# Loading the first 512 tokens' k and v four tokens to a partition, by head pairs, with their retention on 32-row groups of the array and states as 64x64 blocks

## The chip, the cores and the metric

The kernel runs on one core of a Trainium2 chip. The metric is the device time in microseconds (us) of one execution; lower is better. A run of the kernel before takes 208.84 us (median of three). The engines are named as the profile names them: PE is the matrix engine (PEld its weight loads), DVE the vector engine, ACT the scalar engine, POOL the general one, and SP the engine whose queue issues most transfers.

## What is computed

A retention layer (a linear recurrence over tokens) feeds a two-layer block with the Mish activation.

```python
B, H, S, D = 4, 8, 768, 64
gamma = 1.0 - 2.0 ** (-5.0 - np.arange(H))          # one decay per head
for t in range(S):
    state = gamma[None, :, None, None] * state + np.einsum('bhd,bhe->bhde', k[:, :, t], v[:, :, t])
    y[:, :, t] = scale * np.einsum('bhd,bhde->bhe', q[:, :, t], state)
x = y.transpose(0, 2, 1, 3).reshape(B * S, H * D)   # 3072 x 512
h = x @ w_in                                        # 512 x 2048
g = h * tanh(log(1 + exp(h)))
out = g @ w_out                                     # 2048 x 512, float32
```

## The kernel before, in words

**Tiling.** The 3072 tokens are 24 chunks of C = 128 tokens, six to a batch. Within a chunk the recurrence is done in closed form: *scores* (L266, the products of keys and queries), *mask* (L277, keeps the pairs in which the key is not later than the query), *present* (L317, the masked scores times v), *past* (L310, the queries times the state that earlier chunks left), *outer* and *state* (L288, L299, which make the state after the chunk). The powers of gamma are folded into the casts of q and v to float16, by a small constant table `qvs`. The eight heads go as HP = 4 pairs of 64 + 64 dimensions, so that a pair fills 128 partitions.

**Blocks.** The first block is four chunks (512 tokens of batch 0), the ten others are two chunks each. For each block, `g1` (L405) multiplies by w_in and ACT applies Mish; `g2_mm` (L424) or, from the third block of two on, `seven` (L486) multiplies by w_out. While block n is in g1 and g2, the retention of block n+1 is slipped between its matmuls at fixed places (`plan_of`, L646): `scores_two`, `outer_two`, `y_two`.

**States.** The state of a head pair is kept as a 128x128 block, of which only the two 64x64 blocks on the diagonal mean anything. `outer` makes it with one 128x128 matmul for each pair. `state` multiplies by `gcm`, which holds gamma^C in the two diagonal blocks and zero elsewhere, so the cross terms vanish. `past` is one 128x128 matmul for each pair.

**The first block.** Nothing can be put beside it: `first_block` (L570) writes its order out by hand. SP issues, in this order, two halves of q, then k and v of chunks 0 to 3 (eight transfers of 256 KB), then the weights w_in in six pieces (`load_weights`, L550), then w_out. The q of all 512 tokens is loaded four tokens to a partition (`load_first_q`, L177): partition p holds tokens 4p to 4p+3, 1 KB in a row for each head. k and v are loaded one token to a partition, 256 bytes in a row for each head (`load_one`, L120). Then, chunk by chunk, ACT casts k, POOL casts v, PE transposes k (L206), DVE copies the transposes out (L208), PE makes the scores (L273), DVE masks them (L283), and PE makes y (L313, L323) and the outer products (L291), with the state before added by a matmul against the identity (L296); DVE scales the state (L303) and ACT copies y into `xt` (L349, L358). Dummy matmuls (`spin`, L240, and `spin_quarters`, L247) keep PE working where it has nothing to do. After the last chunk come the casts of w_in on DVE (`cast_win`, L152) and then 64 g1 matmuls of 512 columns.

**What sets the order.** The program order on each engine is the order in which the code calls it (`manual_schedule`); an engine does not pass a waiting instruction. PSUM has four one-bank buffers under the tag "mm" and two two-bank buffers under the tag "at"; a new tile waits for the last reader of the tile whose buffer it takes.

The functions that the change touches and what calls them, with the line numbers of the profile:

Of the kernel before, what the change touches and what calls it, by code (L numbers as in the profile page):

```python
# [16 lines left out]
def kernel(  # L17
# [18 lines left out]
    CPB = TB // C  # L36
    BLOCKS = [4] + [2] * ((NCK - 4) // 2)
# [14 lines left out]
    spread = [qs_np[(jj * CPB + r) % C] for r in range(CPB)]  # L52
    qvs_np = np.ascontiguousarray(np.concatenate([qs_np, vs_np, *spread], 1))
# [5 lines left out]
    tpp = ctx.enter_context(tc.tile_pool(name="rn_tp", bufs=2))  # L59
# [12 lines left out]
    qvs = cpool.tile([P, (2 + CPB) * H], FP32, name="qvs")  # L72
    nc.scalar.dma_start(qvs, nc.inline_tensor(qvs_np, name="qvs_c").ap())
    qs, vs = qvs[:, :H], qvs[:, H:2 * H]
    qs_spread = qvs[:, 2 * H:].rearrange("p (r h) -> p h r", r=CPB)
    ident = cpool.tile([P, P], FP16, name="ident")
    tri = cpool.tile([P, C], FP32, name="tri")
    gcm = cpool.tile([P, HP, P], FP32, name="gcm")
# [10 lines left out]
    tri_first = cpool.tile([P, CPB, C // CPB], FP32, name="tri_first")  # L89
    nc.gpsimd.memset(tri_first, 0.0)  # L90
    nc.gpsimd.affine_select(
        out=tri_first, in_=tri_first, compare_op=ALU.is_gt, fill=1.0, base=0,
        pattern=[[-1, CPB], [-CPB, C // CPB]], channel_multiplier=1)
    nc.vector.memset(warm, 0.0)
    nc.scalar.activation(warm, warm, AF.Mish)
    nc.vector.memset(gcm, 0.0)
    for h in range(H):
        o = 64 * (h % 2)
        nc.vector.memset(gcm[o:o + 64, h // 2, o:o + 64], float(gamma[h] ** C))
# [4 lines left out]
    qfirst_t = cpool.tile([P, HP, CPB, P], FP16, name="qfirst_t")  # L104
# [9 lines left out]
    def room(g):  # L114
        loaded[g] = [
            None if nm == "q" and g < CPB else
            lpool.tile([P, H, D], FP32, name=nm + "f", tag=nm + "f", bufs=4 if nm == "q" else 6)
            for nm in "qkv"]
# [33 lines left out]
    def cast_win(s):  # L152
        src = wtmps.pop(("in", s))
        wins[s] = []
        for j in range(2):
            t = cpool.tile([P, NBP, TB // 2], FP16, name=f"win{s}_{j}")
            nc.vector.tensor_copy(t, src[:, :, j * (TB // 2):(j + 1) * (TB // 2)])  # L157
            wins[s].append(t)
# [18 lines left out]
    def load_first_q():  # L177

        qf = wstage.tile([P, H, CPB, D], FP32, name="qfirst", tag="wt", bufs=4)
        for a in range(0, H, H // 2):  # L180
            nc.sync.dma_start(  # L181
                qf[:, a:a + H // 2],
                q[0, a:a + H // 2, :TB].rearrange("h (p r) d -> p h r d", r=CPB))
        return qf

    def turn_first_q(qf, half, on_act):
        a, n = half * (H // 2), H // 2
        q16 = castp.tile([P, CPB, n, D], FP16, name="qfirst16", bufs=1, tag=f"qfirst16_{half}")
        nc.vector.tensor_tensor(
            q16.rearrange("p r h d -> p h r d"), qf[:, a:a + n],  # L190
            qs_spread[:, a:a + n].unsqueeze(3).broadcast_to((P, n, CPB, D)), op=ALU.mult)
        t_ps = mmps.tile([P, n // 2, CPB, P], FP16, name="t_ps", tag="mm")
        for i in range(n // 2):
            for r in range(CPB):
                nc.tensor.transpose(t_ps[:, i, r], q16[:, r, 2 * i:2 * i + 2], ident)
        dst = qfirst_t[:, a // 2:(a + n) // 2]
        if on_act:
            nc.scalar.copy(dst, t_ps)
        else:
            nc.vector.tensor_copy(dst, t_ps)  # L200

    def turn_k(g):
        k16 = cast[g][1]
        t_ps = mmps.tile([P, HP, C], FP16, name="t_ps", tag="mm")
        for i in range(HP):
            nc.tensor.transpose(t_ps[:, i], k16[:, 2 * i:2 * i + 2], ident)  # L206
        kt = qktp.tile([P, HP, C], FP16, name="kt", bufs=2)
        nc.vector.tensor_copy(kt, t_ps)  # L208
        qkts[g] = (qfirst_t[:, :, :, g * (C // CPB):(g + 1) * (C // CPB)], kt)

    def casts(g):
# [4 lines left out]
        if qf is not None:  # L216
            nc.gpsimd.tensor_tensor(  # L217
                q16, qf, qs.unsqueeze(2).broadcast_to((P, H, D)), op=ALU.mult)
# [18 lines left out]
    def at_tile(g):  # L237
        ats[g] = atps.tile([P, 2, HP, C], FP32, name="at", tag="at")

    def spin(g, n):  # L240
        for i in range(0, n, HP):
            m = min(HP, n - i)
            nc.tensor.matmul(  # L243
                ats[g][:, 0, :m], ident, ident.unsqueeze(1).broadcast_to((P, m, P)),
                start=True, stop=True)

    def spin_quarters(g, n, width):  # L247
        for i in range(n):
            r, c = i % 4 // 2, i % 2
            rows = slice(r * D, (r + 1) * D)  # L250
            nc.tensor.matmul(
                ats[g][c * D:(c + 1) * D, r, i // 4 % HP, :width], ident[rows, :D],
                ident[rows, :width], start=True, stop=True, skip_group_check=True)
# [12 lines left out]
    def scores(g):  # L266
        if g not in ats:
            at_tile(g)
        at, (qt, kt) = ats[g], qkts[g]
# [7 lines left out]
    def mask(g, parts=1):  # L277
        am = tpp.tile([P, 2, HP, C], FP16, name="am")
        at = ats.pop(g)
        keep = tri_first.rearrange("p r c -> p (r c)") if g < CPB else tri  # L280
        n = HP // parts
# [123 lines left out]
    def g1(blk, u):  # L405
# [15 lines left out]
        for j in range(per):  # L421
            gts[blk, u * per + j] = gt[:, j]
# [298 lines left out]
```

## Time and profile before

| | |
|---|---|
| runs | 208.76, 208.84 and 210.17 us; median 208.84 us |
| profiled execution, first to last instruction (span) | 206.5 us |
| its own device time | not listed beside the span; the median of the runs is 2.3 us above the span |
| busy: PE, PEld, DVE, ACT, POOL | 200.1, 151.0, 120.7, 86.5, 76.2 us |
| granted clock of PE, mean | 0.999 |
| k of chunks 0 to 3 landed, so that ACT could start its cast, at | 8.11 (behind other work of ACT), 10.36, 12.77, 15.13 us |
| first g1 matmul | 19.49 us |
| first matmul by w_out | 33.55 us |

Times inside an execution are counted from its first instruction. A line of the timeline has the start, the time, the engine, the line of the kernel, the operation, the tile written and those read, the shapes and the count; in brackets stands how long the engine had been idle and what ended that. The chain is the sequence of work that ended last, followed back from the last instruction. A matmul's time in a group is from its start to the end of its pipeline, so that a row of matmuls started one after another overlaps; the chain counts from the end of one group to the end of the next.

### The profile page before, as it was taken

The page shows a single profiled execution, that of the slowest core. Times are in us where ns is not written, and L with a number is a line of the kernel's source. Part 1 is how long each engine was busy: PE and PEld are TensorE (multiplying, and loading weights), DVE is VectorE, ACT ScalarE, POOL GpSimd, SP SyncE. Part 2 cuts the span into 40 slices and gives each one's busy share as a digit, 9 for nine tenths or more (in the row PEclk, how much of TensorE's full clock was granted, in tenths as well). Part 3 has the DMA queues.
Part 4 walks back from the last instruction along what each step waited for, and adds up shares of the span by engine and source line. Part 5 has one row for each costly group of instructions (what it writes and reads, how often), then busy time and mean ns, then how long its engine had stood idle before and what let it go on. Part 6 is the DMA issues. An engine that isn't in the chain of part 4 may idle for free.

```text
span 206.5 us, 4747 instructions
## 1 busy us (share of the span) xinstructions
PE 200.1 (97%) x2005; PEld 151.0 (73%) x2005; DVE 120.7 (58%) x184; ACT 86.5 (42%) x146; POOL 76.2 (37%) x72
## 2 busy tenths in 40 slices
PE   7899999999999999999999999999999999999993
PEld 2465444455855865788888888888888888898882
DVE  2697454267019998475585774495675773572062
ACT  2243664142631541453453453453453453552640
POOL 3242000427866555578665265156266000000000
PEclk9999999999999999999999999999999999999999
DMA  5999999999899999999999798499894800200202
GB/s 175 237 219 345 381 387 355 233 296 208 176 205 292 195 228 207 213 238 253 209 218 152 168 195 149 115 246 154 200 241 71 206 0 2 105 0 27 77 25 76
DMA packets 99988, 38.59 MB, mean 187 GB/s; under 512 B 90496, under 2 KB 94080, under 8 KB 99968
## 3 DMA queue, kind: packets, MB, share of 16 engines
q1 hardware_dynamic: 96704, 37.50, 82.4%
q10 hardware_dynamic: 3264, 0.81, 2.4%
q8 instruction: 15, 0.25, 0.5%
q14 instruction: 5, 0.04, 0.1%
HBM read 27.29 MB, written 6.29 MB: 163 GB/s over the span
## 4 chain that ended last, share of the span: by engine, by line
PE 83%; SPq 7%; DMA 5%; DVE 1%; ACT 1%; issue 1%; ACTq 0%
PE h_ps L412 38%; PE o_ps L506 23%; PE o_ps L426 13%; SPq L122 5%; DMA wi<-in_moe_w_in_dram 5%; PE y_ps L323 3%; PE at L273 3%; PE y_ps L313 2%; SPq L140 2%; PE u_ps L291 2%; ACT xt L400 1%; DVE gsum L476 1%; SPq L181 0%; DVE win L157 0%; PE t_ps L261 0%
## 5 line engine op out<-in xcount | busy, mean ns | idle before, releaser
L412 PE MATMUL h_ps<-xt,win 128*128 128x256 f16 (+1 forms) x704 | 88.0, 282 | 0.4 <-ACT xt L400 0.2
L420 ACT ACTIVATE g<-h_ps 128x512 f16<-128x512 f32 x96 | 57.3, 597 | 57.6 <-PE h_ps L412 57.6
L412 PEld LDWEIGHTS <-win 128*128 128x128 f16 x704 | 67.9, 98 | 16.9 <-DVE win L157 0.9
L217 POOL TENSOR_TENSOR qk<-qf,qvs 128x512 f16<-128x512 f32 x20 | 21.5, 1077 | 61.6 <-DMA qf<-in_q_dram 52.3
L283 DVE TENSOR_TENSOR am<-at,tri 128x1024 f16<-128x1024 f32 x20 | 23.7, 1220 | 17.1 <-PE at L273 16.9
L223 POOL TENSOR_TENSOR v<-vf,qvs 128x512 f16<-128x512 f32 x24 | 25.4, 1059 | 18.6 <-DMA vf<-in_v_dram 17.0
L426 PE MATMUL o_ps<-wout,g 128*128 128x512 f16 x128 | 30.1, 380 | 0.0
L222 POOL TENSOR_SCALAR qk<-kf 128x512 f16<-128x512 f32 x18 | 27.7, 1540 | 2.0 <-DMA kf<-in_k_dram 0.7
L506 PEld LDWEIGHTS <-gsum 128*128 128x128 f16 x256 | 24.4, 98 | 3.8 <-DVE gsum L476 0.4
L506 PE MATMUL o_ps<-tmat,gsum 128*128 128x256 f16 x192 | 23.7, 273 | 0.1
L426 PEld LDWEIGHTS <-g 128*128 128x128 f16 x128 | 11.7, 98 | 13.0 <-issue 0.3
L520 DVE TENSOR_TENSOR osb<-o_ps,snap 128x256 f32<-128x256 f32 x24 | 10.1, 422 | 18.8 <-ACT snap L512 15.7
L506 PEld LDWEIGHTS <-g 128*128 128x128 f16 x192 | 18.8, 98 | 2.2
L400 ACT CAST xt<-y_ps 128x1024 f16<-128x1024 f32 x10 | 10.1, 1012 | 21.7 <-PE y_ps L323 21.7
L475 DVE TENSOR_TENSOR gsum<-g 128x512 f16<-128x512 f16 x16 | 7.6, 472 | 13.6 <-ACT g L420 13.6
L506 PE MATMUL o_ps<-wout,g 128*128 128x256 f16 x128 | 15.3, 273 | 0.0
L512 ACT COPY snap<-o_ps 128x256 f32<-128x256 f32 x24 | 8.9, 372 | 14.0 <-PE o_ps L506 14.0
L306 DVE TENSOR_TENSOR su<-u_ps,st 128x512 f32<-128x512 f32 x13 | 9.0, 691 | 4.7 <-PE u_ps L291 4.5
L307 DVE TENSOR_TENSOR st<-su,gcm 128x512 f16<-128x512 f32 x13 | 9.8, 754 | 0.4
L243 PE MATMUL at<-ident 128*128 128x512 f16 (+1 forms) x26 | 8.0, 440 | 1.3 <-POOL ident L81 1.3
L220 ACT ACTIVATE qk<-kf 128x512 f16<-128x512 f32 x6 | 3.8, 630 | 12.4 <-DMA kf<-in_k_dram 12.4
L157 DVE CAST win<-wi 128x1024 f16<-128x1024 f32 x8 | 5.4, 692 | 5.3 <-DMA wi<-in_moe_w_in_dram 5.3
(61 smaller groups left out, 150.0 us busy)
## 6 DMA issues: line engine op xcount, KB each, us to landing
kf<-in_k_dram SPq DMA_DIRECT2D x23, 256.0 KB, 4.9
vf<-in_v_dram SPq DMA_DIRECT2D x23, 256.0 KB, 5.0
out_dram<-osb SPq DMA_DIRECT2D x22, 256.0 KB, 4.0
qf<-in_q_dram SPq DMA_DIRECT2D x19, 256.0 KB, 4.4
wt<-in_moe_w_out_dram SPq DMA_DIRECT2D x3, 1024.0 KB, 10.1
wi<-in_moe_w_in_dram SPq DMA_DIRECT2D x4, 512.0 KB, 6.9
wi<-in_moe_w_in_dram SPq DMA_DIRECT2D x2, 1024.0 KB, 10.3
qfirst<-in_q_dram SPq DMA_DIRECT2D x2, 512.0 KB, 5.0
```

The costliest lines, as they stand in the source:

```text
L122: queue.dma_start(loaded[g][n], (q, k, v)[n][b, :, c * C:(c + 1) * C].rearrange("h p d -> p h d"))
L217: nc.gpsimd.tensor_tensor(q16, qf, qs.unsqueeze(2).broadcast_to((P, H, D)), op=ALU.mult)
L222: nc.gpsimd.tensor_scalar(k16, kf, BOOST, None, op0=ALU.mult)
L223: nc.gpsimd.tensor_tensor(v16, vf, vs.unsqueeze(2).broadcast_to((P, H, D)), op=ALU.mult)
L283: nc.vector.tensor_tensor(am[:, :, i:i + n], at[:, :, i:i + n], keep.unsqueeze(1).unsqueeze(1).broadcast_to((P, 2, n, C)), op=ALU.mult)
L307: nc.vector.tensor_tensor(st, su, gcm, op=ALU.mult)
L400: nc.scalar.copy(xt[:, :, :2 * C], y_ps.rearrange("p i j c -> p i (j c)"))
L412: nc.tensor.matmul(h_ps[:, j], wins[s][f // 2][:, bp, f % 2 * P:(f % 2 + 1) * P], xts[blk][:, bp, :nt], start=(bp == 0), stop=(bp == NBP - 1))
L420: nc.scalar.activation(gt, h_ps, AF.Mish, scale=inv_boost3)
L426: nc.tensor.matmul(o_ps, gts[blk, fb][:, t * P:(t + 1) * P], wouts[s][:, f, cols], start=(fb == 0), stop=(fb == NFB - 1))
L506: nc.tensor.matmul(o_ps, x(f), w(f), start=first and f == 0, stop=f == n - 1, skip_group_check=True)
L520: nc.vector.tensor_tensor(dst, o_ps, plus, op=ALU.add)
```

## The change

The k and v of the first 512 tokens are loaded as q was: four tokens to a partition. All twelve transfers (q, k and v for each of four head pairs) are now 256 KB with rows of 1 KB, in the order q0 k0 q1 k1 v0 v1 q2 k2 v2 q3 k3 v3. The work of the first block goes by head pairs and halves of two pairs, no longer by chunks. A chunk of 128 tokens now lies in 32 partitions (tokens 4p to 4p+3 of 32 partitions), so its matmuls contract over 32 rows of the array at a time, in four steps r. `tri_first` becomes a table over two of these indices. From the first block on, the state of a head pair is two 64x64 blocks, side by side in the partitions: `outer` and `past` become two matmuls of 64 columns of weights for each pair, `gcm`, `st` and `su` are half as wide, and `past` uses 64 rows and 64 columns of the array at a time. `spin_quarters` goes; `spin` has other counts. The first two units of g1 are split in halves (`g1_part`), the first half ahead of the second half of y; the first of the w_in casts goes to ACT. The diff, cut:

```diff
+    Q0 = C // CPB
...
-    gcm = cpool.tile([P, HP, P], FP32, name="gcm")
+    gcm = cpool.tile([P, HP, D], FP32, name="gcm")
...
+    tri_first = cpool.tile([P, CPB, CPB, Q0], FP32, name="tri_first")
     nc.gpsimd.memset(tri_first, 0.0)
+    for c in range(CPB):
+        t = tri_first[c * Q0:(c + 1) * Q0]
+        nc.gpsimd.affine_select(
+            out=t, in_=t, compare_op=ALU.is_gt, fill=1.0, base=0,
+            pattern=[[1, CPB], [-1, CPB], [-CPB, Q0]], channel_multiplier=CPB)
...
-    def outer(g, u_ps, onto=None):
+    def outer(g, u_ps):
         _, k16, v16, _ = cast[g]
         for i in range(HP):
-            nc.tensor.matmul(
-                u_ps[:, i], k16[:, 2 * i:2 * i + 2], v16[:, 2 * i:2 * i + 2],
-                start=onto is None or i == 0, stop=onto is None,
-                skip_group_check=onto is not None)
+            for hh in range(2):
+                nc.tensor.matmul(
+                    u_ps[64 * hh:64 * hh + 64, i], k16[:, 2 * i + hh], v16[:, 2 * i + hh],
+                    start=i == 0, stop=True, skip_group_check=True)
...
     def past(g, y, fresh, pairs=range(HP)):
         st, qt = states[g - 1], qkts[g][0]
         for i in pairs:
-            nc.tensor.matmul(
-                y(i), st[:, i], qt[:, i], start=fresh(i), stop=False,
-                skip_group_check=True)
+            for hh in range(2):
+                o = slice(64 * hh, 64 * hh + 64)
+                nc.tensor.matmul(
+                    y(i)[o], st[o, i], qt[o, i], start=fresh(i), stop=False,
+                    skip_group_check=True)
...
+    def g1_part(h_ps, u, part):
+        for bp in range(2 * part, 2 * part + 2):
+            nc.tensor.matmul(
+                h_ps[:, 0], win(0, u, bp), xts[0][:, bp], start=(bp == 0), stop=(bp == NBP - 1),
+                skip_group_check=True)
...
+    def first_loads():
+        for nm, i in (("q", 0), ("k", 0), ("q", 1), ("k", 1), ("v", 0), ("v", 1),
+                      ("q", 2), ("k", 2), ("v", 2), ("q", 3), ("k", 3), ("v", 3)):
+            t = lpool.tile([P, 2, CPB, D], FP32, name=nm + "f", tag=nm + "f", bufs=4 if nm == "q" else 6)
+            nc.sync.dma_start(
+                t, dict(q=q, k=k, v=v)[nm][0, 2 * i:2 * i + 2, :TB].rearrange(
+                    "h (p r) d -> p h r d", r=CPB))
...
+    def score_pair(i, at, parts=1):
+        for hh in range(2):
+            o = slice(64 * hh, 64 * hh + 64)
+            for r in range(CPB):
+                for c in range(CPB):
+                    nc.tensor.matmul(
+                        at[rows(c), hh, r], qkt2[i][o, 1, r, rows(c)],
+                        qkt2[i][o, 0, :, rows(c)], start=True, stop=True,
+                        skip_group_check=True)
...
+    def state_half(half):
+        u_ps = [mmps.tile([P, 2, 2, D], FP32, name="u_ps", tag="mm") for _ in range(2)]
+        pairs = slice(2 * half, 2 * half + 2)
+        for c in range(CPB):
+            if c % 2 == 0:
+                for cc in (c, c + 1):
+                    for j in range(2):
+                        for r in range(CPB):
+                            for hh in range(2):
+                                i = 2 * half + j
+                                nc.tensor.matmul(
+                                    u_ps[cc % 2][64 * hh:64 * hh + 64, cc // 2, j],
+                                    qk16[i][rows(cc), 1, r, hh], v16p[i][rows(cc), r, hh],
+                                    start=cc < 2 and j == 0 and r == 0, stop=r == CPB - 1,
+                                    skip_group_check=True)
...
+            if c > 0:
+                nc.tensor.matmul(
+                    u, ident, states[c - 1][:, pairs], start=False, stop=True,
+                    skip_group_check=True)
+            nc.vector.tensor_tensor(states[c][:, pairs], u, gcm[:, pairs], op=ALU.mult)
+            yield
+
+    def y_half(half, y, off, cs, fresh, eng):
...
+        for j in range(2):
+            for c in cs:
+                for r in range(CPB):
+                    for hh in range(2):
+                        i = 2 * half + j
+                        nc.tensor.matmul(
+                            at(c, j)[64 * hh:64 * hh + 64], v16p[i][rows(c), r, hh],
+                            amp[i][rows(c), hh, r], start=fresh and j == 0 and r == 0,
+                            stop=c == 0 and r == CPB - 1, skip_group_check=True)
+        for j in range(2):
+            for c in cs:
+                if c > 0:
+                    for hh in range(2):
+                        i, o = 2 * half + j, slice(64 * hh, 64 * hh + 64)
+                        nc.tensor.matmul(
+                            at(c, j)[o], states[c - 1][o, i], qkt2[i][o, 0, :, rows(c)],
+                            start=False, stop=True, skip_group_check=True)
...
+    def first_retention():
+        at = at_tile()
+        spin(at, 72)
+        cast_pair("q", 0, nc.vector)
+        cast_pair("k", 0, nc.scalar)
+        turn_pair("q", 0, nc.vector)
+        turn_pair("k", 0, nc.scalar)
+        spin(at, 4)
+        cast_pair("q", 1, nc.vector)
+        cast_pair("k", 1, nc.scalar)
+        for i in range(2):
+            cast_pair("v", i, nc.gpsimd)
+        turn_pair("q", 1, nc.vector)
+        score_pair(0, at)
+        turn_pair("k", 1, nc.scalar)
+        at = at_tile()
+        spin(at, 4)
+        score_pair(1, at)
+        cast_pair("q", 2, nc.gpsimd)
+        cast_pair("k", 2, nc.scalar)
+        at = at_tile()
+        spin(at, 8)
+        chain = state_half(0)
+        next(chain)
+        next(chain)
+        turn_pair("k", 2, nc.scalar)
+        y = y_tile()
+        y_half(0, y, 0, (0, 1), True, nc.scalar)
+        next(chain)
+        cast_pair("v", 2, nc.gpsimd)
+        cast_pair("q", 3, nc.gpsimd)
+        cast_pair("v", 3, nc.gpsimd)
+        cast_pair("k", 3, nc.scalar)
+        turn_pair("q", 2, nc.vector)
+        next(chain)
+        score_pair(2, at)
+        turn_pair("k", 3, nc.scalar)
+        y_half(0, y, 2 * C, (2, 3), False, nc.scalar)
+        at = at_tile()
+        spin(at, 4)
+        turn_pair("q", 3, nc.vector)
+        score_pair(3, at, 2)
+        chain = state_half(1)
+        next(chain)
+        next(chain)
+        next(chain)
+        cast_win(0, 0, nc.scalar)
+        h_ps = [mmps.tile([P, 1, TB], FP32, name="h_ps", tag="mm") for _ in range(2)]
+        for u in range(2):
+            g1_part(h_ps[u], u, 0)
+        y_half(1, y_tile(), 0, (0, 1), True, nc.scalar)
+        y_half(1, y_tile(), 0, (2, 3), True, nc.vector)
+        next(chain)
+        return h_ps
```

`cast_pair` casts one head pair of q, k or v to float16 (k always on ACT); `turn_pair` transposes one pair of q or k in four steps on PE and copies the result out; `score_pair` ends with the mask on DVE, one instruction of 1024 elements or, for the last pair, two of 512; `y_half` ends with the copy of y into `xt`.

## The prediction, before the run

> **What bounds the kernel now.** I read the first page, then the chain in order of time, then the timeline of the first 26 us, then the groups. The page says that PE is the bound over the whole span, and that the granted clock is at its full nine tenths or more in every slice:
>
> ```profile
> span 206.5 us, 4747 instructions
> PE 200.1 (97%) x2005; PEld 151.0 (73%) x2005; DVE 120.7 (58%) x184; ACT 86.5 (42%) x146; POOL 76.2 (37%) x72
> ```
>
> The chain shows two regimes. Up to 26 us it consists of transfers, and from there of PE work, with hardly a gap:
>
> ```profile
> 16.44 9.41 DMA wi<-in_moe_w_in_dram
> 25.88 0.70 DVE win L157
> 26.63 7.08 PE h_ps L412 x32
> ...
> 60.92 0.55 PE at L273 x16
> 61.47 1.83 PE o_ps L426 x8
> 63.30 0.45 PE u_ps L291 x8
> 63.75 1.73 PE o_ps L426 x8
> 65.48 0.22 PE y_ps L313 x4
> 65.70 0.59 PE y_ps L323 x16
> ```
>
> The last six lines give a price that this change needs. Eight o_ps matmuls take 1.73 us behind u_ps, which uses the whole array as they do, and 1.83 us behind the scores, which use half-height tiles: going back costs 0.10 us. Going into tiles costs as much again: y_ps L323 is 8 rounds of two tiles side by side, 8 x 0.056 = 0.45 us by the pace of u_ps L291 (0.45/8), and takes 0.59 or, mostly, 0.57 us. So each change of the tile shape costs about 0.1 us of PE, and from here on PE has nothing to hide it under.
>
> The timeline of the first block:
>
> ```profile
> 10.36 0.63 ACT L220 ACTIVATE qk<-kf 128x512 f16<-128x512 f32 x1 [1.62 <-DMA kf<-in_k_dram]
> ...
> 11.38 0.58 PE L251 MATMUL at<-ident 64*64 64x64 f16 x48
> ...
> 12.42 1.22 DVE L283 TENSOR_TENSOR am<-at,tri_first 128x1024 f16<-128x1024 f32 x1
> ...
> 12.77 0.63 ACT L220 ACTIVATE qk<-kf 128x512 f16<-128x512 f32 x1 [1.78 <-DMA kf<-in_k_dram]
> ...
> 15.13 0.63 ACT L220 ACTIVATE qk<-kf 128x512 f16<-128x512 f32 x1 [1.25 <-DMA kf<-in_k_dram]
> ...
> 16.25 0.42 PE L251 MATMUL at<-ident 64*64 64x128 f16 x16
> ...
> 18.74 0.69 DVE L157 CAST win<-wi 128x1024 f16<-128x1024 f32 x1 [0.16 <-DMA wi<-in_moe_w_in_dram]
> ...
> 19.49 6.87 PE L412 MATMUL h_ps<-xt,win 128*128 128x512 f16 x31
> ```
>
> ACT waits for each k: 2.4 us from one to the next, so a chunk's k and v take 1.2 us a transfer. But DVE has little slack beside that: it is busy 4.40 and 3.96 us of the stretches 10 to 15 and 15 to 20 us. Faster transfers alone would soon meet it.
>
> **Transfers.** The two halves of q, with rows of 1 KB, let DVE start at 5.26 and 6.76 us: 1.5 us for 512 KB, so 0.75 to 0.78 us for each of the twelve new transfers. From q0 at about 4.5 us on, v3 lands near 13.0 us and the first piece of w_in (pieces come 1.48 us apart) near 14.5 instead of 18.7 us. That is 4.2 us won on the queue, if anything waits for it.
>
> **The new first block.** I take the new program order and the durations of the rows. DVE: 1024 elements 1.22 us, 512 0.69, 256 0.42 (L283, L303, L520), so 128 elements about 0.28; a copy of 512 transposed values 0.42. ACT: cast of k 0.63, copy of 512 0.57. POOL: 1.06 for a cast. A hop costs 0.05 us, and 0.22 us pass from the last matmul's start to its end. PE: a round of tiles of 128 columns 0.056 us; 48 small matmuls of 64 columns in 0.58 us, four at a time, are 0.032 us a round; a change of shape puts 0.15 us between two starts instead of 0.056. A pair's scores (32 matmuls, four column tiles at a time) are then 7 rounds and last 0.66 us to their end, since the next row half overlaps the last round; 32 outer products are 15 rounds, 0.73 us; a quarter of y 13 rounds and the past behind them, 1.15 to 1.3 us. The same arithmetic on the old order puts the first g1 matmul at 19.6 us, against 19.49 in the trace.
>
> Now the path. 72 dummy columns instead of 54 end at 7.1 us. Transposes of q0, copy on DVE to 7.98, and only behind it on DVE the cast of q1, to 8.66. Transposes of q1; scores of pair 0, in order behind them, 9.03 to 9.69; mask 9.73 to 10.95. The transposes of k1 stand behind scores 0 on PE, so scores 1 run 10.67 to 11.33 and their mask to 12.59. The state of chunk 0 is queued behind that mask on DVE (to 12.87), and PE stands at the identity matmul of chunk 1, with everything for pairs 2 and 3 queued behind it. The first quarter of y ends at 14.45, the outer products of chunks 2 and 3 at 15.1; two more hops DVE to PE bring scores 2 to 16.04 and their mask to 17.96. The dummy in that mask's buffer holds back the transposes of q3 to 18.35. Copy to 19.20, scores 3 to 19.91, two half masks to 21.30, three state hops to 22.98 with four g1 matmuls between, the third quarter of y to 24.45, the last to 25.64, its copy on DVE to 26.37. The other 60 g1 matmuls start at 26.42 us. At 0.216 us each, with 0.1 us for the second cast of w_in, they end at 39.5 us, where w_out's first matmul stood at 33.55: 5.9 us later. PE and DVE wait for each other in turn, and no transfer is on the path any more.
>
> What costs nothing: the casts on POOL (the last ends at 14.1 us, used at 19.8); the larger triangle on POOL, five instructions that start by 2 us and are needed at 9.7; the ACT cast of w_in (done by 19.9, used at 22.5); ten of SP's issues, which stay ahead of use. The w_out transfers wait for w_in's casts, so they are issued at 27.4 instead of 20.95 us; with the weights of w_in landed before that, their 3 us of transfer still fit ahead of 39.5 us.
>
> **The other ten blocks.** `past` keeps its number of rounds (pairs on the two diagonal tiles, 8 x 0.056 = 0.45 us), but the whole-array shape becomes 64x64, and `present` behind it is again another shape: one change more, 0.12 us with its slow first round, ten times, 1.2 us. `outer` goes from 8 whole-array matmuls (0.45 us) to 8 rounds of 64 columns in tiles: with 0.032 us a round and two changes 0.47 us, with 0.056 us 0.66. Four of the ten have one chunk only: 0.22 becomes 0.34 to 0.44 us. That is +0.6 to +2.2 us in all; I take +0.8, nearest the row of 64 columns. DVE's su and st halve (0.69 and 0.75 to about 0.42 us), which gains nothing: no wait of PE in this stretch ended on them. Sum: 5.9 + 1.2 + 0.8 = 7.9 us. Against the profiled span of 206.5 us that is 214.4; the median of the runs lies 2.3 us above the span, so 216.7 us.
>
> [...]
>
> **Rivals.** *Cheap tiles.* Rounds on 32-row groups overlap more (no row of before has that shape), and a change between tile shapes costs nothing. With halved rounds and no change cost the same path ends at 23.1 us, 3.3 earlier, and the other blocks lose nothing: 206.5 + 2.6 + 2.3 = 211.4 us. For it: scores and outer products lie in several row groups. Against it: the next tile's turn comes only after the four steps r of one tile, and matmuls start in order.
>
> *The past runs one by one.* Its two tiles of a pair write one bank of PSUM. Everything in before that uses two row halves (L273, L251) writes two banks, so no row shows this. Serial, 16 rounds instead of 8 cost 0.45 us seven times and 0.22 three times: +3.8 us, about 220.5 us. [...]
>
> *Transfers stay the bound (faster).* If the new path kept up with them, g1 would start one cast (0.69) and two hops after the first w_in at 14.5, at 15.3 us, 4.2 earlier: 206.5 - 4.2 + 2.0 + 2.3 = 206.6 us. For it, the 2.4 us steps of the chain are transfers. It decides only if y is done by 18.5 us (no change) or 16.4 us (1% faster); but DVE alone has 10.0 us of work from 7.56 us on (four copies 1.7, a cast 0.7, the masks 5.0, seven states 2.0, a copy of y 0.7), which ends at 17.6 without a single wait; and PE's own work with its changes of shape (transposes 1.8, scores 2.3, outer products 2.7, identity 1.2, y 4.4, dummies 1.0, g1 0.9 us) ends past 21 us.
>
> **Numbers.** Forecast (214 to 219 us) 0.60; cheap tiles, whole or in part (210.9 to 214 us), 0.20; one by one 0.08; transfers the bound 0.07; about no change by some of both 0.05. The range 210.9 to 220.8 reaches over cheap tiles and one by one and leaves out 0.12 to 0.2. One per cent, 2.1 us, is about what a measurement of this kernel tells from no change: faster 0.07, same 0.05, slower 0.88.
>
> **What would show it.** In the new profile: k casts of ACT no longer waiting for transfers past 11 us; the first w_in landed by 15 us and idle for some us; the second g1 parts near 26 us; PE waits ended by masks and states in between; y_ps L615 and L270 behind a gap of 0.15 us. If the first block ends before 18.5 us I am wrong on the hops; if PE's `past` takes 0.9 us for 16, on the bank.

## The result and the profile after

| | before | after |
|---|---|---|
| median of the runs | 208.87 us | 224.58 us (223.83 to 225.27) |
| profiled execution: device time, span | span 206.5 us | 225.27 us, 223.4 us |
| busy: PE, DVE, ACT, POOL | 200.1, 120.7, 86.5, 76.2 us | 213.5, 111.1, 87.8, 83.3 us |
| mean granted clock | 0.999 | 0.947 |
| second part of the first g1 group / first g1 matmul before | 19.49 us | 32.50 us (forecast: 26.42) |
| first matmul by w_out | 33.55 us | 48.15 us (forecast: 39.5) |
| from there to the end of the span | 172.95 us | 175.25 us (forecast: 174.95) |

The ratio of after to before is 1.075, with a 95% interval of 1.071 to 1.079: 15.7 us slower, where 7.9 were forecast. The direction was right, and so was nearly everything behind the first w_out matmul; the first block was not. It costs 14.6 us instead of 5.9.

The lines of the page of after (the granted clock is the row PEclk, 5.6 us to a digit):

```profile
span 223.4 us, 5449 instructions
PE 213.5 (96%) x2349; PEld 155.4 (70%) x2349; DVE 111.1 (50%) x186; ACT 87.8 (39%) x148; POOL 83.3 (37%) x77
...
PE   7889789999999999999999999999999999999994
...
PEclk9975556999999999999999999999999999999999
DMA  6999107999989999999939969789399350200202
```

PE is the bound as before, by the first two lines. The row PEclk has what the prediction never asked for: from the third to the seventh slice the clock is below full, and at half in the three in the middle. The row PE shows 7 to 9 tenths in the same slices, so the fall can't be seen there. The view of stretches has it in figures (time, then busy time and instructions of PE, PEld, DVE, ACT and POOL, then the clock, the DMA share, GB/s):

```profile
7.00:14.00 7.00, 5.04 (x122) 2.78 (x121) 4.46 (x6) 2.23 (x4) 5.61 (x6) 1.00 1.08 351
14.00:20.00 6.00, 5.46 (x121) 3.92 (x124) 1.79 (x6) 1.72 (x4) 0.98 (x1) 0.51 1.08 361
...
32.00:38.00 6.00, 5.50 (x13) 1.96 (x14) 4.86 (x9) 1.95 (x4) 0.00 (x0) 0.50 0.52 189
38.00:44.00 6.00, 6.00 (x29) 2.74 (x28) 2.45 (x2) 4.02 (x7) 0.00 (x0) 1.00 0.97 337
```

By the trace's record the clock is full from 7.26 to 14.09 us, 0.5 to 37.98, and full from there. Ahead of 7.26 us the record is empty and the row prints a 9, but there the dummies start 0.43 us apart, twice the 0.216 us of full matmuls of 512 columns: half clock as well. PE starts at 1.34 us in before and in after, yet the first release came at 4.77 us in the one and at 7.26 in the other (4.38 to 7.26 us over all traces). So the dummies in front (72 units of 128 columns) end at 8.30 us in after, where 7.1 was forecast. A busy PE is no PE at its pace: 13 matmuls in the six us of the third line, 29 in those of the last. The timeline of the first block:

```profile
8.39 2.52 POOL L537 TENSOR_TENSOR v<-vf,qvs 128x512 f16<-128x512 f32 x2 [2.68 <-DMA vf<-in_v_dram]
...
8.91 1.08 DVE L537 TENSOR_TENSOR qk<-qf,qvs 128x512 f16<-128x512 f32 x1
...
10.38 0.46 PE L559 MATMUL at<-qkt 64*32 64x128 f16 x32
...
14.71 1.08 PE L606 MATMUL y_ps<-am,v 32*64 32x128 f16 x32
...
18.18 1.23 PE L559 MATMUL at<-qkt 64*32 64x128 f16 x32 [0.36 <-DVE qkt L551]
...
23.68 0.72 PE L582 MATMUL u_ps<-v,qk 32*64 32x64 f16 x25
...
25.24 0.37 PE L582 MATMUL u_ps<-v,qk 32*64 32x64 f16 x7 [0.84 <-issue]
...
32.50 1.89 PE L361 MATMUL h_ps<-xt,win 128*128 128x512 f16 x4 [0.57 <-DVE xt L626]
```

Three things are to be seen. The 32 scores take 0.46 us at full clock (0.66 on record) and 1.23 at half, a stop of 0.40 us behind the tenth of them included (0.68 at half without a stop, in the run with w_in held). The cast of q on DVE takes 1.08 us beside POOL's casts, not 0.69. And between 25 and 7 of 32 outer products, which wait for nothing new, PE stands for 0.84 us with "issue" as the reason: nothing that the profile shows. None of PE's waits up to here ends on a transfer, as forecast.

The chain of after in the second block, against the six lines shown of before:

```profile
76.35 0.55 PE at L234 x16
76.91 1.83 PE o_ps L367 x8
78.74 0.37 PE u_ps L249 x16
79.11 1.83 PE o_ps L367 x8
80.94 0.34 PE y_ps L270 x8
81.28 0.59 PE y_ps L280 x16
```

The outer products (L249) became 0.08 us shorter and the group behind them 0.10 longer; past (L270) went from 0.22 to 0.34: the price of one more change of shape, about 0.12 as forecast.

### The profile page after: what moved, and what is told of

It reads as the page before. It is cut to its first block, busy times and chain, and to the rows that moved or that the text cites. A ratio compares the mean times of both kernels' runs of the same rounds, so it can differ in the third digit from the quotient of the medians.

```text
span 223.4 us, 5449 instructions
## 1 busy us (share of the span) xinstructions
PE 213.5 (96%) x2349; PEld 155.4 (70%) x2349; DVE 111.1 (50%) x186; ACT 87.8 (39%) x148; POOL 83.3 (37%) x77
## 4 chain that ended last, share of the span: by engine, by line
PE 89%; DMA 3%; DVE 3%; ACT 2%; issue 1%; POOL 0%; POOLq 0%; DVEq 0%; ACTq 0%
PE h_ps L354 38%; PE o_ps L447 21%; PE o_ps L367 9%; PE at L213 3%; DMA kf<-in_k_dram 3%; PE y_ps L280 3%; PE at L234 3%; PE y_ps L270 2%; PE y_ps L606 2%; PE h_ps L361 2%; PE u_ps L249 1%; PE t_ps L547 1%; PE u_ps L582 1%; PE at L559 1%; ACT xt L327 1%
## 5 line engine op out<-in xcount | busy, mean ns | idle before, releaser
L187 POOL TENSOR_TENSOR qk<-qf,qvs 128x512 f16<-128x512 f32 x20 | 22.5, 1126 | 85.5 <-DMA qf<-in_q_dram 72.4
L193 POOL TENSOR_TENSOR v<-vf,qvs 128x512 f16<-128x512 f32 x20 | 21.3, 1067 | 2.3 <-DMA vf<-in_v_dram 0.9
L213 PE MATMUL at<-ident 128*128 128x512 f16 x23 | 8.9, 541 | 1.3 <-POOL ident L84 1.3
L417 DVE TENSOR_TENSOR gsum<-gsum,g 128x512 f16<-128x512 f16 x16 | 8.6, 540 | 0.5
L447 PE MATMUL o_ps<-wout,gsum 128*128 128x256 f16 x64 | 8.3, 272 | 0.0
L447 PE MATMUL o_ps<-tmat,g 128*128 128x256 f16 x64 | 8.3, 272 | 0.0
L373 DVE COPY osb<-o_ps 128x512 f32<-128x512 f32 x8 | 5.3, 686 | 5.1 <-PE o_ps L367 3.4
```

Source lines behind the costliest of these rows:

```text
L187: nc.gpsimd.tensor_tensor(q16, qf, qs.unsqueeze(2).broadcast_to((P, H, D)), op=ALU.mult)
L193: nc.gpsimd.tensor_tensor(v16, vf, vs.unsqueeze(2).broadcast_to((P, H, D)), op=ALU.mult)
L213: nc.tensor.matmul(at[:, 0, :m], ident, ident.unsqueeze(1).broadcast_to((P, m, P)), start=True, stop=True)
L447: nc.tensor.matmul(o_ps, x(f), w(f), start=first and f == 0, stop=f == n - 1, skip_group_check=True)
```

## The experiments

The first theory was that the clock fell because TensorE had too little to do, and that this was the larger part of the loss. The rival was that small tiles and hops are dear by themselves. The order below is that of the reasoning.

**Fillers in the idle stretches** (92 units of 128 columns, in eight places of the first block; the expectation says 88):

```
+def fill(at, n):
+    for i in range(0, n, HP):
+        nc.tensor.matmul(at[:, 0], ident,
+            ident.unsqueeze(1).broadcast_to((P, HP, P)), start=True, stop=True)
...
 spin(at, 4)
+fill(at, 12)
 score_pair(1, at)
```

> The changed kernel, with matmuls on the full array (ident by ident, each 512 columns wide, written to tiles of PSUM that are written anew afterwards) put into TensorE's idle stretches of the first block: 88 units of 128 columns in all. They feed nothing. Theory 1 (the granted clock was halved because TensorE had too little to do in a stretch of the first block, and that halving is the larger part of the loss): the clock stays at 1.0 from its release to the end, the second parts of the g1 group start at 25.0 to 26.5 us instead of 32.50, the 56 g1 matmuls run at full rate, and the time is 214.5 to 216.5 us. Rival (the small tiles and the added hops cost the time by themselves, and the clock is only a by-product): the fillers can only add to the first block, the second parts of g1 start at 32 us or later, and the time is 224 us or more.

Measured: 222.60 us (ratio 1.069, 1.063 to 1.074). The clock was at 0.5 from 25.21 to 28.62 us only, and yet 2 us were won, not 8 to 10. Neither side had this right. PE now stood still twice, for longer than in after:

```profile
17.22 0.22 PE L597 MATMUL u_ps<-st,ident 128*128 128x128 f16 x1 [1.55 <-issue]
...
23.69 0.46 PE L588 MATMUL u_ps<-v,qk 32*64 32x64 f16 x23 [2.11 <-issue]
```

The second is again in the middle of a group. Counting PE's instructions in order of start (a weight load and a matmul each, and two of the sequencer at the head), the stops lie behind number 449 and number 705, and that of after behind 705 too: 256 apart. The page lists a queue for instructions, and one answer on the DMA of after between 22 and 24 us has one packet of it:

```profile
q8 instruction: 18, 0.29, 0.6%
```

```profile
q8 instruction: 1, 0.02, 3.4%
```

18 packets of 0.29 MB are 16 KB each, for 2349 matmuls of PE and as many weight loads; before has 15 for 2005. In the trace, the packet ahead of each stop starts 2.4 to 2.7 us before PE goes on. So a second theory: PE ran out of instructions, because the packet with the next 256 stands in line behind the loads.

| kernel | packet starts | PE reaches the end of its block | it goes on |
|---|---|---|---|
| before | 13.87 / 20.71 | 16.91 / 40.01 | at once / at once |
| after | 16.14 / 22.62 | 18.37 / 24.16 | 18.77 / 25.24 |
| fillers | 14.84 / 21.10 | 15.30 / 21.40 | 17.22 / 23.69 |
| fillers, w_in later | 14.87 / 18.61 | 15.20 / 23.85 | 17.49 / at once |
| fillers, all of w_in held | 13.11 / 18.05 | 16.55 / 20.93 | within 0.2 / at once |
| before, dummies cut finer | 13.90 / 20.75 | 14.11 / 21.57 | 16.60 / 23.35 |

(First value: number 449, second: 705. Starts of the packets of queue q8, and of PE's instructions, in us.) Before reaches number 705 behind its first block, and 449 3.0 us after the packet started: it just escapes.

**The number of instructions alone, in the kernel before:**

```
-spin_quarters(g + 1, (48, 40, 16)[g], C // 2 if g < 2 else C)
+spin_quarters(g + 1, (112, 104, 16)[g], 16 if g < 2 else C)
```

> The kernel before with two of its groups of dummy matmuls cut finer: 112 and 104 matmuls of 16 columns instead of 48 and 40 of 64 columns. No other instruction changes; TensorE gets 256 instructions more in the first block (a weight load and a matmul each) and 0.6 to 0.8 us more of starts, of which most lies beside its waits. Theory 2: TensorE comes to the end of its block of instructions, number 449, at about 14.5 us instead of 16.9, before the next block is there (about 16.4), and to number 705 at about 18.5 instead of 40, with the next block there at about 22; it stands still for 1.5 us or more at one of the two or both, and the time is 212 to 216 us. Rival (the number of instructions is free): 209.2 to 210.0 us.

Measured: 219.93 us against 208.66 (ratio 1.053, 1.046 to 1.060): 11.3 us for 128 dummy matmuls more (216 of 16 columns in place of 88 of 64), above the expected range.

```profile
13.90 0.38 PE L251 MATMUL at<-ident 64*64 64x16 f16 x25
...
16.60 1.11 PE L251 MATMUL at<-ident 64*64 64x16 f16 x79 [2.32 <-issue]
...
23.35 0.48 PE L273 MATMUL at<-qfirst_t,kt 64*128 64x128 f16 x5 [1.47 <-issue]
```

The first stop cuts a group of dummies that wait for nothing. The clock was 0.5 from 16.84 to 27.08 us. Of the 11.2 us between the two spans (217.64 and 206.47 us), 7.2 lie ahead of the first w_out matmul (40.75 against 33.55 us) and 4.0 behind it: there PE waits 2.41 us for a cast of k, up to 50.66 us, and the clock falls once more, to 54.38 us; why that k came late isn't settled. This kernel has none of the change in it: the finer cut alone cost the 11.3 us.

**The loads ahead of the packet, with fillers.** The second MB of w_in waits for the mask of pair 2, the third and fourth for the first state of the second half:

```
 t = wstage.tile([P, NBP, TB], FP32, name="wi", tag="wt", bufs=4)
+if s in (1, 2):
+    nc.vector.memset(t[:, 0, :1], 0.0)
...
 score_pair(2, at)
+load_w("in", 1)
```

> The changed kernel with the full-array fillers, and the transfers of w_in behind the first MB issued later: the second MB waits for the mask of pair 2, the third and fourth for the first state of the second half (a one-column memset of the target on VectorE makes them wait). TensorE's instructions are the same. With fillers alone TensorE stood still for 1.55 and 2.11 us in the middle of its work, each time at an instruction block's end (instructions 449 and 705 of TensorE, 256 apart), while the packet of the instruction queue that holds the next block started 4 to 6 us after the block before it was begun. Theory 2 (that packet stands in line behind the loads issued before it): with fewer loads in the line both stops shrink below 0.5 us, the clock stays at 1.0 throughout, the second parts of g1 start at 26.5 to 28 us (fillers alone: 31.45), and the time is 217 to 219 us. Rival (the fetch is slow in itself, or the stops are something else): stops of 1.5 to 2.1 us as before, 221.5 to 224 us.

Measured: 221.45 us (ratio 1.059, 1.052 to 1.066), a half answer. The second stop was gone and the first was not (see the table): its packet started at 14.87 us, as the loads then issued ran out (the DMA share falls from 1.10 at 13 to 14 us to 0.18 at 15.0 to 15.5). The clock fell behind that stop, from 18.18 to 25.0 us.

**The same without fillers:**

> The changed kernel without fillers, with the same later transfers of w_in. It takes away the stop for instructions (1.07 us at 24.16 us in the changed kernel, where the clock is at 0.5) and leaves the clock. If the clock is the larger part: it falls to 0.5 again in the first block, the second parts of g1 start at 31 to 32.5 us, and the time is 222.5 to 224.6 us, 0 to 1.5 us less than the changed kernel. If the instruction blocks alone were the cause and the clock only followed them, the clock stays at 1.0 and the time is 217 to 219 us.

Measured: 223.31 us (ratio 1.070, 1.064 to 1.077). The clock fell at 14.62 us, ahead of the stop at 15.30. So stops are not what made it fall.

**All of w_in held back, with fillers.** The first MB waits too, until the mask of pair 1:

```
-if s in (1, 2):
+if s < 3:
...
 score_pair(1, at)
+load_w("in", 0)
```

> As the run with fillers and later transfers, but the first MB of w_in is held back too, until the mask of pair 1 is done. In that run the second stop for instructions had gone and the first (1.92 us) had stayed: its packet started at 14.87 us, when the last load then in the line, w_in's first MB, came to its end. Theory 2 in this form (the packet of instructions starts when the loads issued before it are through): only the 3 MB of q, k and v stand before it now, it starts at 12 to 12.5 us, and the stop at instruction 449 goes too. With no stop and full rows at work the clock stays at 1.0, the second parts of g1 start at 26.2 to 27 us (on record: 26.42), w_out's first matmul at 39.2 to 40 (on record: 39.5), and the time is 217 to 218.5 us. Rival (the first fetch is late for another reason): a stop of 1.5 us or more at instruction 449, the clock falls behind it, 220.5 us or more.

Measured: 219.17 us (ratio 1.051, 1.048 to 1.055). No stop over 0.2 us, and the clock full through the whole first block. The time is below the rival's 220.5 us and 0.7 above the expected range. The packet started at 13.11 us, 0.8 behind number 193 (12.33 us), against 2.2 to 3.9 us in the other kernels of the table. The second g1 parts started at 27.78 us and w_out's first matmul at 40.74, some 0.8 us later than expected. PE's time behind it was 176.5 us, with a wait of 1.36 us for the cast of k of chunk 4 in it.

**The same without fillers: the price of the clock.**

> The same without the fillers: no stop for instructions, and little of the array at work. If the clock falls without any stop: it goes to 0.5 at about 14 us and comes back after 30 us, the second parts of g1 start at 29.5 to 31 us, and the time is 4 to 6 us above the run with fillers, 221.5 to 223.5 us; the difference between the two is the price of the clock alone. If the clock fell in the changed kernel only because of stops and of what they left idle: it stays at 1.0, and the two kernels agree within 1 us.

Measured: 221.78 us (ratio 1.060, 1.054 to 1.065). No stop of PE, and the clock 0.5 from 16.44 to 33.51 us; w_out's first matmul at 44.80 us. The clock alone costs 2.6 us between the medians and 3.7 between the two profiled spans (220.9 and 217.2), less than expected. One reason may be that PE still waits for DVE in the half-clock stretch (0.85 and 0.58 us the longest), and such a wait is no longer there than at full clock; that wasn't tried. The four runs of this kernel point the same way: 219.98 us with a mean clock of 0.984, and 221.75, 221.82 and 222.75 with 0.961.

**What the clock goes by.** Two kernels without dummies or with others. First the kernel before with all dummies behind the first 54 columns' worth removed:

```
-spin(0, 14)
...
-spin(0, 8)
...
-spin(g + 1, 2 if g else 8)
...
-spin_quarters(g + 1, (48, 40, 16)[g], C // 2 if g < 2 else C)
```

> The kernel before with its wide first block, but without any of the dummy matmuls after the first 54 columns' worth, so that TensorE idles between the short groups of the first block; no other instruction is changed. Theory 1 (too little work in a stretch of a few us halves the clock): the clock falls to 0.5 in the first block of the kernel before too, although its tiles are all full, and the time is 5 to 12 us longer, 214 to 221 us. Rival (the halving belongs to the small tiles, not to idle time): the clock stays, and the time is 207.5 to 209.5 us, the same or a little less as the dummies are gone.

Measured: 208.47 us with the clock at 1.0 in the profiled run, and 211.61 us with a mean clock of 0.975 in the other. The first is what the rival expected, the second what neither did. Too little work is at the edge here, not beyond it, though PE was busy for 1.89 of 3.42 us:

```profile
7.04:10.46 3.42, 1.89 (x30) 1.33 (x27) 2.02 (x3) 1.69 (x3) 1.04 (x1) 1.00 1.34 216
```

So idle time alone did not decide it here. Next the fillers on a sixteenth of the array, with and without the stops:

```
-nc.tensor.matmul(at[:, 0], ident, ident.unsqueeze(1).broadcast_to((P, HP, P)), ...
+nc.tensor.matmul(at[:32, 0], ident[:32, :32],
+    ident[:32].unsqueeze(1).broadcast_to((32, HP, P)), ...
```

> The same fillers at the same places with the same number of columns, but on a tile of 32 rows by 32 columns, a sixteenth of the array. If what keeps the clock is the share of time in which TensorE streams columns, the clock stays at 1.0 and the time is that of the run with full-array fillers, 214.5 to 216.5 us. If it is the part of the array that works, the clock falls to 0.5 in the first block as in the changed kernel, and the time is 223 to 226 us. The rival without the clock expects 224 us or more here too, and no difference from the full-array fillers.

Measured: 228.88 us (ratio 1.097, 1.093 to 1.100). The clock fell at 16.95 us and stayed at 0.5 to 40.84: slower than after and than either side expected: the fillers add columns that now run at half clock, and there is a stop at number 449 (17.16 to 18.76 us).

> As the run with all w_in transfers held back and fillers, but the fillers work on 32 rows by 32 columns of the array: the same number of columns at the same places, a sixteenth of the array, and no stop for instructions. If the gate goes by the part of the array that is at work (own count by windows of 3.41 us: it fell behind windows with 0.29 to 0.35 of the array's work, and held with 0.38 and more), the clock falls to 0.5 at 13 to 17 us although TensorE streams columns for 0.7 to 0.8 of the window; the time is 220.5 to 224 us. If it goes by the time in which TensorE streams columns, it stays at 1.0, and the time is 218.5 to 220 us, as with full-array fillers.

Measured: 223.60 us (ratio 1.070, 1.066 to 1.074; the profiled execution took 227.46; the three runs near the median had a mean clock of 0.969 to 0.976, so it fell in them too). There is no stop, PE is busy all the time, and the clock falls:

```profile
13.50:16.90 3.40, 3.40 (x105) 2.13 (x93) 1.52 (x6) 1.70 (x3) 1.47 (x2) 1.00 0.48 143
17.00:20.30 3.30, 3.30 (x72) 1.80 (x71) 1.60 (x3) 0.59 (x1) 0.00 (x0) 0.50 0.49 165
```

The clock's changes lie on a grid of 3.413 us in every trace (in after 14.09 - 7.26 is two of it, 37.98 - 14.09 seven). For each window of that grid one can count the share of time in which at least one tile streams columns ("columns streamed" below), and the columns weighted by their tile's share of the array, rows x columns / 128 x 128 ("share of the array's work"). In after, 10.67 to 14.09 us: 512 columns of transposes, 1536 of dummies, 32 x 128 of scores at 64 x 32 / 128 x 128 = 1/8, 32 x 64 outer products at 1/8: 2816 full columns at 0.417 ns (half of 0.427 us for 512 at half clock), 1.17 us of 3.41, 0.34.

| kernel, window | columns streamed | share of the array's work | clock behind it |
|---|---|---|---|
| small fillers, no stop, 13.52 to 16.94 | 0.77 | 0.29 | falls |
| no fillers, no stop, 13.03 to 16.44 | 0.50 | 0.29 | falls |
| after, 10.67 to 14.09 | 0.45 | 0.34 | falls |
| fillers, 21.80 to 25.21 (a stop in it) | 0.41 | 0.35 | falls |
| before without dummies, 7.04 to 10.46 | 0.38 | 0.38 | holds |
| fillers, 14.97 to 18.38 (a stop in it) | 0.43 | 0.41 | holds |
| before, 11.60 to 15.01 | 0.63 | 0.59 | holds |

The share of the array's work sorts the rows; the columns streamed don't. Counted in the same way over every window of all thirteen traces, the share still sorts them: the clock fell behind 0.35 and less and held behind 0.38 and more. Rows alone don't (fell at 0.56, held at 0.38), nor do columns of the array alone (fell at 0.69, held at 0.39). On the way back, windows with 0.74 and more released the clock, windows with 0.73 and less didn't (after has 0.40 to 0.69 in its six, then 1.00). At 0.74 itself both were seen: the window of after from 0.43 to 3.85 us has 0.74 and released nothing. So shares that kept a full clock did not bring a lost one back: the run with w_in held and fillers went through windows of 0.44 to 0.64 at full clock, and after stayed at half through 0.40 to 0.69. These shares are counted from the trace, and the kernel with 0.38 lost the clock for a while in its other run, so they are what was counted in this case and no rule of the chip.

**The states of the later chunks alone.** The kernel before, with 64x64 outer products, sums and past from chunk 4 on:

```
+if g >= CPB:
+    for hh in range(2):
+        o = slice(64 * hh, 64 * hh + 64)
+        nc.tensor.matmul(y(i)[o], st[o, i], qt[o, i], start=fresh(i), stop=False, ...)
+    continue
```

> The kernel before with its wide first block, and only the states of the later chunks (outer products, sums of states, past) as 64x64 blocks; the last state of the first block is copied out of its two diagonal blocks by two instructions of VectorE. It isolates the second half of the change, at full clock. By the sum on record (shape change and outer, 1.2 + 0.8 us) it is 210.3 to 211.3 us; by what the changed kernel's trace shows behind its first w_out matmul (175.3 against 172.9 us) it is 210.8 to 211.4. The rival of past running one by one on one bank of PSUM gives 214 us or more.

Measured: 211.12 us against 208.92 (ratio 1.011, 1.006 to 1.016), so 2.2 us: the 2.0 on record. One by one on one bank would have been 5.8 (with the rival's 3.8, which no run shows).

**The cast of q beside POOL.** POOL's first cast of v waits for DVE's cast of q of pair 1:

```
 v16p[i] = castp.tile([P, CPB, 2, D], FP16, name="v16")
+if i == 0:
+    nc.vector.memset(v16p[i][:, 0, 0, :1], 0.0)
```

> The run with full-array fillers and all w_in transfers held back, with one order more: GpSimd's first cast of v waits until VectorE has done the cast of q of pair 1 (a one-column memset of its target on VectorE). That cast of q took 1.56 us there, beside GpSimd's cast, and 0.68 us in the runs where GpSimd started behind it; 0.69 was on record. If the two engines slow each other, it takes 0.65 to 0.75 us again, the second parts of g1 start 0.7 to 0.9 us earlier (26.9 to 27.1 instead of 27.78 us), and the time is 218.1 to 218.7 us. If the long cast has another cause (the transfers that land then), it stays at 1.0 us or more and the time at 219.0 to 219.6 us.

Measured: 217.30 us (ratio 1.044, 1.038 to 1.050). The run it builds on, and then this one:

```profile
8.50 1.56 DVE L544 TENSOR_TENSOR qk<-qf,qvs 128x512 f16<-128x512 f32 x1
```

```profile
8.44 0.68 DVE L546 TENSOR_TENSOR qk<-qf,qvs 128x512 f16<-128x512 f32 x1
```

The cast beside no cast of POOL takes 0.68 us; POOL's two casts of v took 2.08 us behind it and 2.52 beside it, so each slows the other. The second g1 parts started at 26.95 us, 0.83 earlier. The other us of the gain came later: the wait of 1.36 us for k of chunk 4 wasn't there (that transfer was awaited for 5.61 instead of 7.37 us by ACT). Why it came sooner isn't settled, and the four runs are spread from 216.49 to 219.01 us.

```profile
span 214.7 us, 5502 instructions
...
PEclk9999999999999999999999999999999999999999
```

This run comes closest to the kernel that the prediction described: a span of 214.7 us where 214.4 was summed, the second g1 parts at 26.95 (26.42), w_out's first matmul at 39.91 (39.5), 174.8 us from there on (174.95). The profiled execution is the fastest of the four; the median is 0.6 us above the forecast of 216.7. And the agreement is in part luck, as two errors cancel: the scores of pair 0 start at 9.98 us where 9.03 was worked out, behind dummies that end at 7.84 (7.1) and three fillers, and the small tiles, quicker than forecast, win back about half of that.

## Why the prediction was wrong

The kernels make a ladder. Each step takes one thing away, from the bottom up:

| kernel | median | span | first w_out matmul |
|---|---|---|---|
| before | 208.9 us | 206.5 us | 33.55 us |
| fillers, w_in held, POOL waits | 217.3 | 214.7 | 39.91 |
| fillers, w_in held | 219.2 | 217.2 | 40.74 |
| w_in held | 221.8 | 220.9 | 44.80 |
| after | 224.6 | 223.4 | 48.15 |

- *The step that failed* is the first term of the sum, "first block 5.9", worked out at "the durations of the rows". Those rows came from an execution of which the prediction said that "the granted clock is at its full nine tenths or more in every slice". That was a fact of before, and it was carried over as if it belonged to the chip. The new front gives the array 0.34 of its work in the window from 10.67 us on, where before never gave it less than 0.59 in its first block; the clock falls, and costs 2.6 us between the medians of the two kernels that differ in the fillers alone (in their profiled executions 3.7 us of span, and 44.80 - 40.74 = 4.06 at the first w_out matmul).
- *What was missing altogether* is the supply of instructions. Up to the second g1 parts PE has 947 instructions in after, up to the first g1 matmul 515 in before, so that number 705 is reached at 24.16 us instead of 40.01. The step from 44.80 to 48.15 us, 3.35, is what holding back w_in takes away: stops of 0.40 and 1.07 us, and a clock that stays at half for 23.9 instead of 17.1 us. How these two share the 3.35 wasn't tried apart. No rival on record had the clock or the supply of instructions in it. At the first w_out matmul the profiled executions account for the whole miss: 3.35 + 4.06 + 0.83 (POOL beside DVE, the next point) + 0.41 that is left = 8.65 us, from 39.5 on record to 48.15.
- *"DVE: ... 512 [elements] 0.69"* held for an engine on its own. Beside POOL's cast the same instruction took 1.08 in after and 1.56 in another run; 0.83 us of the first block in the run where that was tried.
- *Cheap tiles*, the rival of 0.20, was right about the tiles and wrong about the time. At full clock 32 scores take 0.46 us (0.66 on record), 32 outer products 0.59 (0.73), the y quarter's 32 matmuls 0.67 and its past 0.30 to their ends. With these disturbances gone the second g1 parts still come at 26.95, not at 23.1. In the run with w_in held and no fillers PE waits 4.6 us in the first block, and each of these waits ends on DVE or ACT; so the hops between the engines set the end rather than the rounds, a reading that wasn't tried by itself.
- *Past one by one* is out: no run shows the 0.9 us for 16 tiles that it went by; they take 0.56 us in after where 0.45 was before, and the states alone cost 2.2 us.
- *Transfers stay the bound* is out in its own sense: no wait of PE in the first block ended on one. But the loads did hold up PE: the packets with its instructions started later behind them (for numbers 449 and 705 at 14.84 and 21.10 us with fillers, at 13.11 and 18.05 with w_in held as well).
- *The starts of small matmuls* were no limit: 32 scores start within 0.46 - 0.22 = 0.24 us in after, 48 dummies of 64 columns within 0.58 - 0.22 = 0.36 us in before, 8 ns apart in both.
- *The other ten blocks*: 2.0 forecast, 2.3 in after (175.25 - 172.95), with a wait of 0.62 us for k of chunk 4 in it, which nobody forecast.

Long waits of PE were not needed for the clock to fall: it fell with none over 0.55 us in the window ahead of it in the run with w_in held, and with PE busy for 3.40 of 3.40 us in that with small fillers. The step from one block of 256 instructions to the next cost nothing where PE's instructions at hand lasted until 2.4 to 2.7 us behind the start of the next packet; elsewhere the stops were 0.4 to 2.5 us.

## What to carry to other kernels

Before a stretch of full tiles is cut into small ones, price two things that no row of the old profile shows: how much of the whole array is at work in each 3.4 us (here the clock fell to half behind 0.35 and less, and came back only behind 0.74 and more), and how soon PE gets through 256 instructions while the first loads run (here PE goes on 2.4 to 2.7 us behind a packet's start, which comes up to 4.2 us after PE began the block before). A price read at full clock holds only while the new order keeps the clock: 32 scores took 0.46 us at full clock and 0.68 at half. A wait with the reason "issue" in the middle of a group of equal instructions was the sign of the second here (0.84 us in after, 2.11 with fillers), a row PEclk of 5 that of the first.

## What the hardware showed that was not expected

- Matmuls of 16 columns were not free: 128 dummy matmuls more in the kernel before, with fewer columns in all, cost 11.3 us. Two stops for instructions (2.32 and 1.47 us) and the clock behind them made 7.2 us of it ahead of the first w_out matmul; the rest came with a late k.
- The clock fell with PE busy for all of a 3.4 us window (share of the array's work 0.29) and held with PE busy for 1.89 of 3.42 us (0.38). Once lost, it came back only behind 0.74 and more.
- PE's packets of instructions start within some 1 us of numbers 705, 961 and 1217 in before, behind its first block (39.16 against 40.01, 54.39 against 54.78, 69.73 against 69.72 us), and 1.8 to 4.2 us behind numbers 193 and 449 in the first block with its loads (0.8 to 2.3 us there with w_in held back; counted from the first instruction that PE starts behind the number).
- Casts of 512 elements on DVE and POOL side by side: 1.08 to 1.56 us instead of 0.68, and 2.52 instead of 2.08 for POOL's two.
